# Attention with a sliding window, then a mixture of experts: the last tiles of the two expert lists as fixed slots

## Chip, cores, metric

The kernel runs on one core of a Trainium2 chip. The metric is the device time of one execution in microseconds. Engines: TensorE (PE; PEld is its weight load), VectorE (DVE), ScalarE (ACT), GpSimd (POOL), SyncE (SP, which here only issues DMAs).

## What is computed

```python
# q, k, v: [8, 8, 576, 64]; window 32; attention within |i - j| <= 32
scores = where(mask, q @ k.T / 8, -1e9)
x = softmax(scores) @ v              # -> [4608, 512], heads side by side
# mixture of experts: 8 experts, top 1, a bias for each of 2 modalities
logits = x @ w_gate + modality_bias[modality_id]
e_idx = argmax(logits, axis=1)
gate_w = softmax(logits)[e_idx]
for e in range(8):                   # w1[e]: 512 x 1024, w2[e]: 1024 x 512
    m = e_idx == e
    out[m] = gate_w[m] * (relu(x[m] @ w1[e]) @ w2[e])
```

The modality bias is much larger than the spread of `x @ w_gate`, so with these inputs one expert (list A below) gets 2308 rows and one (list B) 2300; the six others get none. The kernel holds for any distribution; it takes the two experts that the biases favour for its two lists.

## The kernel before

Nothing is scheduled by a compiler: the string `ORDER` lists every step of the program in the order in which it is emitted, and each engine executes its own steps in that order. A name is a step, the numbers are its batch and part, `/a`, `/v`, `/p` chooses ACT, DVE or POOL for a copy, and `:n` the PSUM banks.

For each of 8 batches: `l`, `lr`, `lv` load q and k (two groups of four heads, 512 KB each), the remainder rows and v, all but one by SyncE's queue; `c`, `cr`, `cv` cast to bf16; `TQ`, `TK`, `TR` transpose on PE and `tq`, `tk`, `tr` copy out of PSUM; `SA`, `SB` are the scores, `sa`, `sb` the exponentials, `M` the mask on DVE; `V` the product with v and `v` its normalisation into the tile `xt`. `X`, `x`, `L`, `lo`, `B`, `Q`, `E`, `R`, `P` compute the gate and the rank of each row in its expert's list; `Z` (five GpSimd indirect DMAs) scatters the batch's rows to the scratch `scr` in HBM, where each expert has a region of its own. `A` counts, after each batch, whether the two lists have filled another tile of 256 rows, and writes the row number `ri` of the two new tiles, 2b and 2b+1 (or that of a zero region).

`F` fetches a tile of 256 rows from `scr`: SyncE first loads `ri` into a register, then issues the DMA (the first four tiles go to `xg` and are transposed on PE by `N`; the later ones come by a transposing DMA to `xTf`, with a small one for `xm`). `U` (four groups of 8 matmuls) and `u` are the first product and its relu, `D` (two halves of 128 rows, 8 matmuls each) the second, `y` scales by the gate weight on DVE into one of four `ys` buffers, `O` stores rows by a GpSimd indirect DMA; `i` makes its row indices. `W` loads the weights of the two experts, each once.

After the eight batches 16 tiles (0 to 15) are planned, 2048 rows of each list, and 256 + 4 and 252 rows are left. `G`, 34 small DVE steps, makes a table of all remaining tiles of any expert; `J` (eight fills of 272 KB by SyncE's queue) zeroes the rows behind the end of each expert's region. Three more tiles (16, 17, 18) are always run from the table, with `C` before each: weight loads under a condition, on GpSimd's queue. Behind them a branch on the number of tiles in the table skips the code for 22 more. In these runs it is skipped.

Each GpSimd DMA is tracked by one of eight semaphores in turn. The span ends with the framework's own steps: semaphore increments for the DMAs in the skipped code, a drain of each engine, and a clearing of semaphores.

Of the kernel before, what the change touches and what calls it, by code (L numbers as in the profile page):

```python
# [37 lines left out]
tr1.1/v TQ5:7 tq5/v TQ6:2 sa3 lr2.0 TQ7:3 M2 sb3 tq6/v lr2.1 V2:45 tq7/a M3 SA4:67 SB4:01 sa4 l2.1.0 lv2.0 v2
cv1.0/p V3:23 sb4 l2.1.1 SA5:67 v3 cv1.2/p lv2.1 SB5:45 sa5 M4 sb5 X0.0:0 X0.1:1 X0.2:2 lv2.2 X0.3:3 X0.4:6
x0.0/v x0.1/a M5 x0.2/a lv2.3 x0.3/a lv2.4 x0.4/v c1.1.1/p cv1.1/a l3.0.0 c2.0.0/v L0:7 cr2/p c2.0.1/a V4:45  # L40
W0 lo0 l3.0.1 c2.1.0/v TK6:0 V5:12 tk6/a TK7:3 B0.0 lr3.0 TQ8:6 v4 tk7/a TK8:7 I0 TR2:0 tq8/a TQ9:3 B0.1 Q0.0
SA6:45 tk8/a lr3.1 B0.2 v5 TK9:6 E0 sa6 TQ10:7 l3.1.0 B0.3 Q0.1 SB6:12 tr2.0/a B0.4 Q0.2 SA7:45 tr2.1/a tq9/v
cv2.0/p sb6 R0:0 tk9/v TQ11:3 P0.0 sa7 M6 SB7:12 sb7 P0.1 V6:45 P0.4 P0.2 P0.5 tq10/a P0.3 A0.0 SA8:01 Z0.0 v6
tq11/a SB8:67 sa8 c2.1.1/v Z0.1 sb8 l3.1.1 TK10:2 Z0.2 TK11:3 tk10/a tk11/v Z0.3 Z0.4 A0.1 M7 A0.2 V7:45 M8
SA9:01 SB9:67 sa9 A0.3 v7 sb9 l4.0.0 A0.4 X1.0:2 A0.5 X1.1:3 X1.2:0 x1.0/a A0.6 l4.0.1 X1.3:1 x1.1/v X1.4:4
x1.2/a A0.7 x1.3/v x1.4/a M9 lr4.0 L1:5 lo1 cv2.1/p cv2.2/a c3.0.0/a B1.0 TQ12:6 Q1.0 c3.0.1/a TQ13:7 lr4.1 I1
B1.1 V8:23 tq12/v E1 V9:01 lv3.0 tq13/a B1.2 Q1.1 B1.3 SA10:45 Q1.2 TK12:6 cr3/a B1.4 F0 v8 TK13:7 sa10 v9
tk12/a c3.1.0/p R1:2 F1 SB10:34 tk13/a TR3:5 P1.0 sb10 tr3.0/v SA11:01 SB11:67 P1.1 P1.4 lv3.1 P1.2 P1.5
TQ14:2 sa11 P1.3 A1.0 TQ15:3 Z1.0 tr3.1/v N0:4 sb11 tq14/v n0/v Z1.1 tq15/a N1:5 c3.1.1/a Z1.2 U0.0:0 n1/v
cv3.0/a TK14:1 Z1.3 TK15:2 tk14/v U0.1:6 u0.0 Z1.4 tk15/v c4.0.0/a U0.2:7 lv3.2 A1.1 W1 U0.3:3 M10 u0.1 u0.2  # L50
TQ16:4 lv3.3 TQ17:5 A1.2 u0.3 M11 V10:01 Ke tq16/a lv3.4 SA12:67 SB12:23 sa12 A1.3 v10 D0.0.0:4 sb12 V11:67
A1.4 tq17/v SA13:01 c4.0.1/a D0.0.1 A1.5 v11 SB13:23 sa13 TK16:5 A1.6 y0.0 X2.0:6 sb13 X2.1:7 X2.2:0 A1.7
X2.3:1 x2.0/v X2.4:4 x2.1/a x2.2/v TK17:2 D0.1.0:3 x2.3/a x2.4/v tk16/a D0.1.1 M12 tk17/a L2:6 y0.1 lo2 M13 I2
cv3.1/a cv3.2/a U1.0:7 cr4/a F2 B2.0 V12:01 i0 u1.0 B2.1 V13:45 Q2.0 O0.0 l4.1.0 v12 E2 SA14:23 F3 SB14:67
sa14 O0.1 v13 SA15:01 l4.1.1 sb14 lv4.0 SB15:23 B2.2 Q2.1 l5.0.0 TR4:4 B2.3 U1.1:5 Q2.2 sa15 lv4.1 B2.4 M14
l5.0.1 R2:6 U1.2:7 u1.1 P2.0 sb15 tr4.0/v V14:01 P2.1 P2.4 U1.3:5 P2.2 P2.5 u1.2 P2.3 A2.0 SA16:23 Z2.0 v14
lv4.2 tr4.1/a N2:6 u1.3 D1.0.0:7 n2/a Z2.1 SB16:01 N3:4 sa16 Z2.2 U2.0:5 n3/v sb16 U2.1:6 Z2.3 lv4.3 c4.1.0/v
u2.0 D1.0.1 lr5.0 Z2.4 u2.1 TQ18:2 y1.0 TQ19:3 tq18/a U2.2:4 lv4.4 A2.1 tq19/a M15 D1.1.0:0 u2.2 lr5.1 U2.3:1
A2.2 M16 V15:56 u2.3 A2.3 SA17:23 i1 D1.1.1 A2.4 sa17 v15 O1.0 D2.0.0:7 cv4.0/a A2.5 y1.1 SB17:12 X3.0:4
X3.1:3 sb17 A2.6 X3.2:5 x3.0/v O1.1 X3.3:6 X3.4:0 D2.0.1 x3.1/v x3.2/a A2.7 U3.0:4 x3.3/a y2.0 x3.4/a U3.1:1  # L60
M17 u3.0 L3:2 F4 u3.1 i2 U3.2:3 c4.1.1/p lo3 cv4.1/a cv4.2/v D2.1.0:5 B3.0 I3 i3 u3.2 B3.1 F5 Q3.0 O2.0 V16:67
c5.0.0/a c5.0.1/v TK18:0 V17:12 E3 B3.2 tk18/a l5.1.0 v16 TK19:4 TQ20:3 lv5.0 tk19/a D2.1.1 l5.1.1 B3.3 tq20/a
Q3.1 SA18:67 B3.4 lv5.1 TK20:0 y2.1 sa18 TQ21:4 l6.0.0 TK21:3 Q3.2 lv5.2 v17 O2.1 tk20/a R3:5 SB18:67 tq21/a
U3.3:0 P3.0 i4 sb18 lv5.3 P3.1 P3.4 SA19:12 P3.2 U4.0:4 l6.0.1 P3.5 P3.3 u3.3 A3.0 M18 SB19:56 lv5.4 u4.0
D3.0.0:7 sa19 A3.1 U4.1:0 tk21/v Z3.0 lr6.0 sb19 cr5/v V18:12 A3.2 TR5:4 i5 u4.1 D3.0.1 A3.3 v18 Z3.1 tr5.0/a
lr6.1 SA20:56 tr5.1/a U4.2:3 sa20 Z3.2 y3.0 l6.1.0 SB20:01 u4.2 cv5.0/v D3.1.0:4 Z3.3 sb20 U4.3:2 c5.1.0/v
# [42 lines left out]
def kernel(  # L109
# [12 lines left out]
    nc = tc.nc  # L122
# [25 lines left out]
    ctx.enter_context(tc.manual_schedule())  # L148
# [869 lines left out]
```

## Time and profile before

| | |
|---|---|
| median of 3 runs | 308.91 us (305.42 to 310.55) |
| the profiled execution | 306.1 us, its span 304.4 us |
| mean granted TensorE clock | 0.904 |
| PE, DVE, ACT, POOL busy | 230.8, 169.1, 165.7, 106.7 us |
| DMA moved | 55.11 MB |

Durations in the text are from the profiled execution. Windows list the busy time of each engine, TensorE's granted clock, the mean busy share of the 16 DMA engines and GB/s. In a timeline the number in brackets is how long the engine stood idle before an instruction, and behind the arrow is what ended the wait; "issue" means nothing that the profile shows. Lines with SPq, POOLq and so on are those of an engine's sequencer.

### The profile page before, as it was taken

To read this page: it belongs to the slowest core of one execution; us is meant where nothing else is said; L and a number is where in the kernel's file an instruction comes from. 1 tells how busy PE (TensorE), PEld (TensorE's weight loads), DVE (VectorE), ACT (ScalarE), POOL (GpSimd) and SP (SyncE) were. 2 spreads that over 40 slices of the span, in tenths; PEclk is the share of its full clock that TensorE was granted. 3 is DMA by queue.
4 is the path that set the end of the run, shared out by engine and by line. 5 is a ranking of instruction groups with operands and counts; after the bars stand their busy time and mean duration, and the time that the engine had idled before them with its cause. 6 is when DMAs were issued, how large, how long until landed. Compare 5 with 4: busy or idle time off the path is not lost. (4 is left out here: it accounts for less than half of the span.)

```text
span 304.4 us, 6737 instructions
## 1 busy us (share of the span) xinstructions
PE 230.8 (76%) x2497; PEld 165.1 (54%) x2497; DVE 169.1 (56%) x486; ACT 165.7 (54%) x287; POOL 106.7 (35%) x150
## 2 busy tenths in 40 slices
PE   0087785671897989996996995999999399999700
PEld 0065573561775667764773773677756166666300
DVE  7168887852587467865874774677651742321200
ACT  0396978574497478859885974675331133233100
POOL 6012264516402513372135236131447422322300
PEclk9999978657699799999999799799999789999955
DMA  5999999999998965999999642062055887410110
GB/s 172 211 266 261 261 245 203 289 301 218 236 197 228 323 164 124 257 304 320 231 212 302 167 89 105 37 91 86 34 96 148 296 269 140 138 73 32 75 40 1
DMA packets 95171, 55.11 MB, mean 181 GB/s; under 512 B 68851, under 2 KB 90651, under 8 KB 95131
## 3 DMA queue, kind: packets, MB, share of 16 engines
q1 hardware_dynamic: 85835, 35.42, 52.6%
q0 software_dynamic: 8624, 18.66, 21.6%
q10 hardware_dynamic: 672, 0.53, 0.5%
q8 instruction: 21, 0.34, 0.5%
q14 instruction: 19, 0.16, 0.2%
HBM read 50.49 MB, written 18.04 MB: 225 GB/s over the span
## 5 line engine op out<-in xcount | busy, mean ns | idle before, releaser
L803 PE MATMUL banks<-xTf,w 128*128 128x256 bf16 x608 | 79.3, 280 | 5.1 <-issue 5.0
L809 ACT ACTIVATE hT<-banks 128x512 bf16<-128x512 f32 x76 | 45.1, 601 | 63.9 <-PE banks L803 53.1
L816 PE MATMUL banks<-w,hT 128*128 128x512 bf16 x304 | 76.3, 386 | 2.4 <-ACT hT L809 1.9
L830 POOL DMA_INDIRECT out_dram<-ys,ix x38 | 39.2, 1033 | 96.2 <-DVE ys L823 24.7
L803 PEld LDWEIGHTS <-w 128*128 128x128 bf16 x608 | 59.0, 100 | 18.0 <-issue 5.5
L522 ACT ACTIVATE pt<-banks 128x768 bf16<-128x768 f32 x64 | 50.7, 823 | 18.3 <-PE banks L514 14.8
L676 POOL DMA_INDIRECT scr<-xt,di x40 | 41.7, 1042 | 35.6 <-issue 29.9
L823 DVE TENSOR_SCALAR ys<-banks,xm 128x512 f32<-128x512 f32 x30 | 22.5, 750 | 46.0 <-PE banks L816 31.0
L816 PEld LDWEIGHTS <-hT 128*128 128x128 bf16 x304 | 28.3, 99 | 31.3 <-ACT hT L809 3.8
L482 PE MATMUL banks<-ident,cb 128*128 128x128 bf16 x256 | 25.9, 260 | 25.0 <-ACT cb L187 23.4
L536 DVE TENSOR_TENSOR pt<-pt,mask 128x1920 bf16<-128x1920 bf16 x32 | 36.8, 1151 | 1.8 <-ACT pt L525 1.8
L482 PEld LDWEIGHTS <-cb 128*128 128x128 bf16 x256 | 20.4, 118 | 30.2 <-ACT cb L187 24.1
L514 PE MATMUL banks<-qT,kT 64*128 64x192 bf16 (+1 forms) x320 | 24.6, 263 | 7.7 <-DVE kT L189 2.4
L550 PE MATMUL banks<-vt,pt 128*128 128x65 bf16 x320 | 24.9, 205 | 5.9 <-DVE pt L536 4.6
L550 PEld LDWEIGHTS <-pt 128*128 128x128 bf16 x320 | 23.1, 106 | 8.7 <-DVE pt L536 5.5
L565 DVE TENSOR_TENSOR xt<-banks,rec 128x640 bf16<-128x640 f32 x32 | 26.4, 824 | 1.6 <-DVE rec L564 0.4
L555 PE MATMUL banks<-vt,pt 128*128 128x65 bf16 x256 | 23.8, 205 | 0.0
L514 PEld LDWEIGHTS <-kT 64*128 64x128 bf16 x320 | 12.6, 101 | 16.9 <-issue 11.0
L555 PEld LDWEIGHTS <-pt 128*128 128x128 bf16 x256 | 20.4, 105 | 0.6 <-issue 0.5
L187 ACT CAST cb<-qkf 128x1024 bf16<-128x1024 f32 x17 | 17.6, 1063 | 2.6 <-DMA qkf<-in_k_dram 1.5
L187 ACT COPY kT<-banks 128x512 bf16<-128x512 bf16 (+1 forms) x29 | 15.3, 554 | 4.6 <-PE banks L482 3.5
L189 DVE COPY qT<-banks 128x512 bf16<-128x512 bf16 (+1 forms) x16 | 9.7, 610 | 14.4 <-PE banks L482 12.4
(159 smaller groups left out, 231.0 us busy)
## 6 DMA issues: line engine op xcount, KB each, us to landing
w<-in_moe_w_dram POOLq DMA_DIRECT2D x10, 1024.0 KB
qkf<-in_q_dram SPq DMA_DIRECT2D x16, 512.0 KB
vf<-in_v_dram SPq DMA_DIRECT2D x32, 256.0 KB
qkf<-in_k_dram SPq DMA_DIRECT2D x15, 512.0 KB
scr<-zero SPq DMA_DIRECT2D x9, 272.0 KB
xg<-scr SPq DMA_DIRECT2D x4, 272.0 KB
rf<-in_q_dram SPq DMA_DIRECT2D x8, 128.0 KB
rf<-in_k_dram SPq DMA_DIRECT2D x8, 128.0 KB
```

The lines of the kernel that those rows point to most:

```text
L187: nc.scalar.copy(o_ap, i_ap)
L482: nc.tensor.transpose(tp[:, i, :], Ct["c", b, hp // 2, u][:, i, D * l_:D * l_ + P], ident[:])
L514: nc.tensor.matmul(st[:, h, c0:c0 + w_], k_t[b % 2][D * h:D * h + D, hp, P * j:P * j + P], q_t[b % 2][D * h:D * h + D, hp, P * j:P * j + w ...
L522: nc.scalar.activation(p_ap, st[:, :, 0:2 * WIN].rearrange("p h (j c) -> p h j c", c=WIN), ACT.Exp, scale=scale)
L536: masked.append(nc.vector.tensor_tensor(out=p_ap, in0=p_ap, in1=mask[:].unsqueeze(1).to_broadcast([P, 2 * NM, WIN]), op=ALU.mult))
L550: nc.tensor.matmul(o_ap, pt[:, h, SW * m:SW * m + P], vt[:, m, 2 * hp + h, :], start=(m == 0), stop=(m == 0), skip_group_check=True)
L555: nc.tensor.matmul(o_ap, pt[:, h, c1:c1 + P], vt[:, m - 1, 2 * hp + h, :], start=False, stop=True, skip_group_check=True)
L676: ins = nc.gpsimd.indirect_dma_start(out=scr[:], out_offset=bass.IndirectOffsetOnAxis(ap=Ct["di", b][:, m:m + 1], axis=0), in_=x_t[b % 2][ ...
L803: nc.tensor.matmul(ph[:, u, :], w1_sb[t % 2][:, kd, P * mi:P * mi + P], Ct["N", t][1][:, kd, :], start=(kd == 0), stop=(kd == n_kd - 1))
L809: nc.scalar.activation(Ct["h", t][:, 2 * mp:2 * mp + 2, :], Ct["U", t, mp][:, :, :], ACT.Relu)
L816: nc.tensor.matmul(Ct["D", t, s], Ct["h", t][:, kf, P * s:P * s + P], w2_sb[t % 2][:, kf, :], start=(kf == 0), stop=(kf == n_kf - 1))
L830: ins = nc.gpsimd.indirect_dma_start(out=out, out_offset=bass.IndirectOffsetOnAxis(ap=Ct["i", t][:, s:s + 1], axis=0), in_=Ct["y", t, s][: ...
```

## The change

The order is written anew throughout. Six things change beside it.

1. Tiles 16, 17 and 18 become fixed slots: 16 is the next 256 rows of list A, 17 the next of list B, 18 a tile of 128 rows, again of list A. `A` carries list A a second time for it, and ten DVE steps, `H`, make row numbers and penalties. No weights are loaded for them.
2. The table `G` serves only the branch, which is taken if any row is left. Only two fills `J` stand ahead of it; eight more are inside.
3. In the branch, the way taken when no tile is left is laid out differently (`preferred_fallthrough_block`).
4. `k` is a drain of GpSimd. It stands at eight places on GpSimd's queue: ahead of O2.0, Z3.1, the copy I4, O8.0, O10.1, O13.0, O14.0 and O16.0.
5. A one-element exponential on ACT stands at the start (`warm`).
6. In the first batch q and k are loaded ahead of v.

```diff
-Kp0 lv0.0 lr0.0 Kb lv0.1 lr0.1 lv0.2 l0.1.0 Kx cv0.0/a c0.0.0/a lv0.3 l0.1.1 Kp1 Ka TQ0:0 TQ1:1 c0.0.1/a Km Kc
...
-D17.0.0:1 y16.1 C18 D17.0.1 O16.1 D17.1.0:3 y17.0 U18.0:2 O17.0 U18.1:0 u18.0 U18.2:5 u18.1 U18.3:6 u18.2
+Kp0 lr0.0 lr0.1 Kb Kx c0.0.0/a l0.1.0 Kp1 Ka TQ0:0 TQ1:1 tq0/a c0.0.1/p tq1/a l0.1.1 cr0/a Km Kc TK0:2 TK1:3
...
+u17.2 k16 U17.3:6 D16.1.1 u17.3 D17.0.0:4 y16.1 O16.0 U18.0:2 O16.1 U18.1:3 u18.0 D17.0.1 u18.1 D17.1.0:1
...
-    N_TAIL = 3
+    T_A, T_B, T_C = 2 * B, 2 * B + 1, 2 * B + 2
...
+    warm = const.tile([P, 1], FP32)
+    nc.vector.memset(warm[:], 0.0)
+    nc.scalar.activation(warm[:], warm[:], ACT.Exp)
...
     def A(_, b, i):
         if i == 0:
-            nc.vector.tensor_tensor(out=rtile(("cm", b), [P, 2, E])[:], in0=oh_ab[:],
-                                    in1=base[:].unsqueeze(1).to_broadcast([P, 2, E]), op=ALU.mult)
+            nc.vector.tensor_tensor(out=rtile(("cm", b), [P, 3, E])[:], in0=oh_ab[:],
+                                    in1=base[:].unsqueeze(1).to_broadcast([P, 3, E]), op=ALU.mult)
...
     def F_(_, t):
...
+        elif t <= T_C:
+            row_ap = T["rl"][0:1, t - T_A:t - T_A + 1]
+            deps = [i_ for _, i_ in scr_ins] + fill_ins + zp_ins
         else:
-            row_ap = T["tab"][0:1, 2, t - 2 * B:t - 2 * B + 1]
-            deps = [i_ for _, i_ in scr_ins] + fill_ins + zp_ins if t < 2 * B + N_TAIL else None
+            row_ap = T["tab"][0:1, 2, t - T_C - 2:t - T_C - 1]
+            deps = None
         r_r = reg(row_ap, [ET.SP], 0, ZP)
-        rows = scr[bass.ds(r_r, TT), :]
+        ns = 1 if t == T_C else 2
+        rows = scr[bass.ds(r_r, P * ns), :]
...
     def U(_, t, mp):
-        ph = bank([P, 2, TT])
-        for u in range(2):
-            mi = 2 * mp + u
+        nu, w_ = (4, P) if t == T_C else (2, TT)
+        ph = bank([P, nu, w_])
+        for u in range(nu):
+            mi = nu * mp + u
             for kd in range(n_kd):
-                nc.tensor.matmul(ph[:, u, :], w1_sb[t % 2][:, kd, P * mi:P * mi + P], Ct["N", t][1][:, kd, :],
-                                 start=(kd == 0), stop=(kd == n_kd - 1))
+                nc.tensor.matmul(ph[:, u, :], w1_sb[t % 2][:, kd, P * mi:P * mi + P],
+                                 Ct["N", t][1][:, kd, 0:w_], start=(kd == 0), stop=(kd == n_kd - 1))
...
+    def last_tiles():
+        ca = Ct["ca", B - 1]
+        end_i = const.tile([P, 2], I32)
+        nc.vector.tensor_tensor(out=end_i[:], in0=row_ab[:, 0:2], in1=ca[:, 0:2], op=ALU.add)
...
+        T["rl"] = rl
...
+        T["pl"] = pen_l
...
+    op["H"] = lambda _, i_: next(last_steps)
...
+    def fill(row_ap):
+        r_e = reg(row_ap, [ET.SP], 0, ZP - TT)
+        return nc.sync.dma_start(scr[bass.ds(r_e, TT), :].rearrange("(s p) c -> p s c", p=P), zero[:])
...
+    op["k"] = lambda _, i_: nc.gpsimd.drain()
...
-    with tc.If(n_tiles > N_TAIL, preferred_fallthrough_block=False):
-        for t in range(2 * B + N_TAIL, 2 * B + NTILE):
-            tile_alone(t)
+    with tc.If(n_tiles > 0, preferred_fallthrough_block=True):
+        for e in range(E):
+            fill(T["ends"][0:1, e:e + 1])
+        for i_ in range(NTILE):
+            tile_alone(T_C + 2 + i_)
```

How the instructions move at three places (x4 behind a row is a run of equal rows). SyncE's queue at the start of the program, before: q of the first four heads, then v and the remainder rows (`rf`) in turn, then q and k of the other four heads. (k of the first four goes by ACT's queue in both kernels.)

```order
L225 DMA qkf<-in_q_dram 128x4x256
L265 DMA vf<-in_v_dram 128x8x64
L241 DMA rf<-in_q_dram 64x8x64
L265 DMA vf<-in_v_dram 128x8x64
L241 DMA rf<-in_k_dram 64x8x64
L265 DMA vf<-in_v_dram 128x8x64
```

And now:

```order
L226 DMA qkf<-in_q_dram 128x4x256
L242 DMA rf<-in_q_dram 64x8x64
L242 DMA rf<-in_k_dram 64x8x64
L226 DMA qkf<-in_q_dram 128x4x256
L226 DMA qkf<-in_k_dram 128x4x256
L307 DMA mid_106<-in_moe_modality_id_dram 8x96
L308 DMA mid_106<-in_moe_modality_id_dram 24x1x128
L309 DMA mid_106<-in_moe_modality_id_dram 8x96
L266 DMA vf<-in_v_dram 128x8x64 x4
```

All loads of v moved behind q, k and the modality ids.

SyncE's queue around the fetch of tile 0, the first that reads `ri`; before, q, k and remainders of batch 3 stand ahead of it (the last rows before it):

```order
L225 DMA qkf<-in_q_dram 128x4x256
L225 DMA qkf<-in_k_dram 128x4x256
L241 DMA rf<-in_q_dram 64x8x64
L241 DMA rf<-in_k_dram 64x8x64
L265 DMA vf<-in_v_dram 128x8x64
L182 TENSOR_LOAD ri
L755 ISA
L755 DMA xg<-scr 128x2x272
```

And now:

```order
L226 DMA qkf<-in_q_dram 128x4x256
L226 DMA qkf<-in_k_dram 128x4x256
L266 DMA vf<-in_v_dram 128x8x64 x3
L183 TENSOR_LOAD ri
L771 ISA
L771 DMA xg<-scr 128x2x272
```

The q and k here are the second half of batch 2, so the fetch of tile 0 moved ahead of all of batch 3.

GpSimd's queue at the branch, before: if it isn't taken, the engine falls into the increments (ISA) and then jumps over the code of the 22 tiles.

```order
L830 DMA out_dram<-ys,ix 4608x512 x5
L984 TENSOR_LOAD tab
L986 COMPARE_AND_BRANCH
L986 ISA
L986 UNCONDITIONAL_BRANCH
L182 TENSOR_LOAD tab x2
```

And now, with the last two rows of the branch's code and what follows it:

```order
L851 DMA out_dram<-ys,ix 4608x512 x2
L1055 UNCONDITIONAL_BRANCH
L1055 ISA
L1055 UNCONDITIONAL_BRANCH
L1085 ISA
```

The increments moved behind the code of the tiles: the jump over it comes first.

More of the change, by code (lines that the diff above doesn't have):

```diff
@@ L38 @@
[L38 to L42, printed above, removed]
@@ L422 @@
     ext_e = const.tile([P, NTILE + 2], FP32)
-    oh_ab = const.tile([P, 2, E], FP32)
-    row_ab = const.tile([P, 2], FP32)
+    oh_ab = const.tile([P, 3, E], FP32)
+    row_ab = const.tile([P, 3], FP32)
     sp_i = const.tile([P, 2], I32)
+    df = const.tile([P, 1], FP32)
     @named
@@ L450, in Kx @@
                                 scalar2=None, op0=ALU.add)
-        nc.vector.tensor_scalar(out=row_ab[:], in0=ext_e[:, 0:2], scalar1=float(LP), scalar2=None, op0=ALU.mult)
+        nc.vector.tensor_scalar(out=row_ab[:, 0:2], in0=ext_e[:, 0:2], scalar1=float(LP), scalar2=None, op0=ALU.mult)
         nc.vector.tensor_copy(sp_i[:], ext_e[:, 0:2])
@@ L847, in table @@
         dn = const.tile([P, E], FP32)
-        nc.vector.tensor_scalar(out=thr[:], in0=thr[:], scalar1=-float(TT), scalar2=None, op0=ALU.add)
-        yield
-        nc.vector.tensor_tensor(out=dn2[:], in0=oh_ab[:], in1=thr[:].unsqueeze(2).to_broadcast([P, 2, E]), op=ALU.mult)
+        nc.vector.tensor_tensor(out=dn2[:], in0=oh_ab[:, 1:3, :],
+                                in1=T["th"][:, 1:3].unsqueeze(2).to_broadcast([P, 2, E]), op=ALU.mult)
         yield
@@ L952 @@
     op["G"] = lambda _, i_: next(steps)
+    def fill(row_ap):
+        r_e = reg(row_ap, [ET.SP], 0, ZP - TT)
+        return nc.sync.dma_start(scr[bass.ds(r_e, TT), :].rearrange("(s p) c -> p s c", p=P), zero[:])
     @named
     def J(_, e):
-        r_e = reg(T["end"][0:1, e:e + 1], [ET.SP], 0, ZP - TT)
-        ins = nc.sync.dma_start(scr[bass.ds(r_e, TT), :].rearrange("(s p) c -> p s c", p=P), zero[:])
+        ins = fill(T["end"][0:1, e:e + 1])
         unordered(ins, "scr")
```

200 lines of the change are left out of this document (122 added, 78 removed).

## The prediction

> **What bounds the kernel now.** I read the page first, then the windows, the timelines of the stretches where TensorE stands still, and last the rows of the end.
>
> ```profile
> PE 230.8 (76%) x2497; PEld 165.1 (54%) x2497; DVE 169.1 (56%) x486; ACT 165.7 (54%) x287; POOL 106.7 (35%) x150
> ...
> 20.00:40.00 20.00, 14.75 (x213) 11.77 (x212) 17.49 (x31) 16.85 (x29) 3.84 (x5) 1.00 1.12 262
> 60.00:80.00 20.00, 10.02 (x112) 8.23 (x113) 7.64 (x25) 10.53 (x17) 10.69 (x23) 0.63 1.14 268
> ...
> 110.00:115.00 5.00, 5.00 (x56) 3.50 (x55) 4.31 (x11) 3.45 (x8) 0.95 (x1) 1.00 0.13 31
> 170.00:175.00 5.00, 5.00 (x58) 3.93 (x57) 3.15 (x14) 4.24 (x9) 1.16 (x2) 0.91 0.37 105
> 235.00:240.00 5.00, 2.03 (x11) 0.90 (x10) 2.69 (x8) 0.60 (x1) 3.78 (x5) 0.91 0.99 295
> 240.00:245.00 5.00, 2.49 (x8) 0.85 (x8) 4.52 (x22) 2.06 (x4) 0.41 (x1) 0.50 0.68 254
> 290.00:295.00 5.00, 0.00 (x0) 0.00 (x0) 0.00 (x0) 0.00 (x0) 0.00 (x0) 0.53 0.09 34
> ...
> 283.67 3.40 PE L816 MATMUL banks<-w,hT 128*128 128x512 bf16 x15
> ```
>
> The window rows give PE, PEld, DVE, ACT, POOL, then granted clock, DMA share and GB/s. TensorE is busy for 230.8 of 304.4 us, so 73.6 us are idle, and the question is where they lie. They have four homes. Up to 15.8 us nothing has reached TensorE. From there to 170 us, where their share falls to 0.37, the DMA engines are the limit (1.12 and 1.14 in the two windows shown), except around 110 us, where their share falls to 0.13 while loads are still outstanding. After 170 us TensorE is nearly always busy, except in 235 to 245 us: 4.5 of 10. Behind the last matmul, which ends near 287.1 us, come some 17 us without any engine. The profiled execution took 306.1 us, 1.7 beyond its span and 2.8 below the median of 308.91.
>
> **The end.** These are instructions of GpSimd's sequencer.
>
> ```profile
> 288.13 0.97 POOL L830 DMA_INDIRECT out_dram<-ys,ix  x1 [0.69 <-DVEq L986]
> ...
> L986 POOLq EVENT_SEMAPHORE  x5: 17/43/43, 288.6 to 291.5; - x5
> L986 POOLq INC_SWDGE_SEM  x1: 1847/1847/1847, 292.1 to 292.1; - x1
> L986 POOLq COMPARE_BRANCH  x2: 41/44/48, 288.5 to 294.0; - x2
> ...
> L1013 POOLq DRAIN  x3: 46/103/6903, 296.7 to 304.1; - x3
> L1002 POOLq DRAIN  x1: 183/183/183, 0.5 to 0.5; - x1
> ...
> scr<-xt,di POOLq DMA_INDIRECT x40
> out_dram<-ys,ix POOLq DMA_INDIRECT x38
> w<-in_moe_w_dram POOLq DMA_DIRECT2D x10, 1024.0 KB
> wg_sb<-in_moe_w_gate_dram POOLq DMA_DIRECT2D x1, 8.0 KB
> ```
>
> The last store is issued at 288.1 and has landed by 291.5; then 1.85 us in INC_SWDGE_SEM, a jump at 294.0 and nothing until 296.7, and a drain of 6.9 us. The data are long in memory by then: it is not a transfer that this drain waits for. A drain with nothing before it takes 0.18 us, and the two behind the long one at most 0.10. So I read it as bookkeeping for each DMA that GpSimd issued since the last drain: 40 + 38 + 10 and one for the gate weights make 89, that is 78 ns each (83, if six weight loads that their condition skipped don't count). The changed kernel drains eight times on the way, the last time behind the stores of tile 15, with five stores to follow: 5 x 78 = 0.4 us, **6.5 saved** (bounds: nothing, if the drain has a fixed price, and 6.9). If INC_SWDGE_SEM walks the same list, it falls to about 0.5, 1.3 saved (0 to 1.8). The jump's 2.6 us now come before the wait for the last landing instead of behind it, and that wait is 2.4 us long (289.1 to 291.5): 2.0 saved (0 to 2.6). Together **-9.8**, between 0 and -11.3.
>
> The Trainium skill ("Runtime: NRT & Kernel Launch", "Instruction fetch mechanics") says that a taken branch to a page outside the fetch window must first fetch it; the 2.6 us behind the jump agree. By that rule alone both kernels make one far jump and the 2.0 would be lost, a sum 2.0 us higher; I keep it, since the new one has a wait to hide behind.
>
> **The half tile.** Of 2308 and 2300 rows, 16 tiles take 2048 each. What is left, 256 + 4 and 252, was three tiles of 256 and becomes two, and one of 128.
>
> ```profile
> 279.09 3.66 PE L803 MATMUL banks<-xTf,w 128*128 128x256 bf16 x32
> 275.64 3.62 PE L816 MATMUL banks<-w,hT 128*128 128x512 bf16 x16
> L482 PE MATMUL banks<-ident,cb 128*128 128x128 bf16 x256 | 25.9, 260 | 25.0 <-ACT cb L187 23.4 <-DVE cb L189 1.2 <-POOL cb L191 0.4
> 45.02 0.62 PE L482 MATMUL banks<-ident,cb 128*128 128x128 bf16 x8
> 276.71 0.05 POOL L722 DMA_DIRECT2D w<-in_moe_w_dram  x1 [2.95 <-DMA w<-in_moe_w_dram]
> ```
>
> The second product drops 8 of 16 matmuls: 1.8 us. The first keeps 32, on 128 columns instead of 256. A pair of that size comes every (0.62 - 0.26) / 7 = 51 ns (the group's mean of one, 260 ns, for the first), so 1.7 to 1.9 us instead of 3.66. **-3.6**, in a stretch where TensorE has no idle time; its price if the weight loads don't keep up is bounded by no gain on the first product, -1.8. The weight loads that were skipped by condition cost GpSimd a wait of 2.95 us, but TensorE's matmuls go on across it: 0.
>
> The Trainium skill ("TensorE: Matmul & The Clock Gate", "Back-to-back issue gap") gives about 81 ns for such a pair in a sustained stream; its estimate would be 32 x 81 = 2.6 us, and the term -2.9. The row of this trace is faster than that, and decides.
>
> **The stall at 235 us.**
>
> ```profile
> 237.86 9.30 SPq L958 DMA_DIRECT2D scr<-zero  x8
> 240.73 0.37 PE L803 MATMUL banks<-xTf,w 128*128 128x256 bf16 x1 [1.83 <-issue]
> 235.79 0.75 DVE L823 TENSOR_SCALAR ys<-banks,xm 128x512 f32<-128x512 f32 x1 [6.08 <-DMA out_dram<-ys,ix]
> ```
>
> Eight fills of 272 KB go out in 9.3 us. In the same stretch TensorE issues the matmuls of one group with over a microsecond between them and waits for nothing visible, as if its instructions came late over the full DMA engines, and DVE waits 6.1 us for a `ys` buffer, because the stores stand behind GpSimd's scatters. Two fills remain, and the table's 34 DVE steps no longer precede a fetch. The scatters stay in front of the stores. Of 5.5 idle us I take 3.5 back: **-3.5** (0 to -5.5).
>
> **The first phase.**
>
> ```profile
> 12.48 1.28 ACT L187 ACT_TABLE_LOAD   x1 [12.48 <-DMA vf<-in_v_dram]
> ...
> 14.73 1.99 ACT L187 CAST cb<-qkf 128x1024 bf16<-128x1024 f32 x2
> 15.82 1.98 PE L482 MATMUL banks<-ident,cb 128*128 128x128 bf16 x16 [15.82 <-ACT cb L187]
> ...
> 4.00:6.00 2.00, 0.00 (x0) 0.00 (x0) 1.61 (x12) 0.00 (x0) 1.86 (x9) 1.00 0.99 324
> 6.00:8.00 2.00, 0.00 (x0) 0.00 (x0) 1.81 (x12) 0.00 (x0) 0.52 (x3) 1.00 1.23 291
> ...
> 56.77 0.17 DVE L701 TENSOR_SCALAR ri<-ro 128x2 int32<-128x2 f32 x1
> 69.42 3.95 SPq L755 DMA_DIRECT2D xg<-scr  x2
> 75.86 1.04 PE L785 MATMUL banks<-ident,xg 128*128 128x128 bf16 x8 [6.42 <-DMA xg<-scr]
> ...
> 106.82 0.70 SPq L241 DMA_DIRECT2D rf<-in_k_dram  x1
> 115.33 0.16 DVE L701 TENSOR_SCALAR ri<-ro 128x2 int32<-128x2 f32 x1
> 116.39 1.37 SPq L760 DMA_TRANSPOSE xTf<-scr  x1
> ```
>
> ScalarE's first work is a cast of v, whose loads land at 12.5; only then do the table load, that cast and the q cast follow. Now q and k come first, 1.05 MB, and at the 290 to 320 GB/s of 4 to 8 us they are there near 8; the table load lies ahead of them. First transposes near 9 instead of 15.8: 6.8 us. The row of tile 0 is known at 56.8, but its fetch stands behind four more q and k loads and their remainders in SyncE's queue and starts at 69.4; TensorE waits 6.4 us for it. In the new queue only three v loads separate it from the loads of its own batch's successor. Around 110 us the queue stands for 9.6 us at the fetch of tile 4, until DVE has made its row number at 115.3, with no load behind it going out.
>
> None of these three adds up freely, since the DMA engines set this stage: a TensorE that starts 6.8 us earlier meets the same arrival of v, and a fetch put forward pushes a load back. What can stay is expert work done inside the phase. The new order holds one batch fewer of loads ahead of the fetch of tile 4, so the queue can run dry there again. Of 6.8 + 6.4 + 9.6 = 22.8 I take about a quarter: **-6**; bounds +6 (a prefetch too shallow, three more stops of about 2 us) and -21.
>
> **The drains on the way.**
>
> ```profile
> 284.68 0.97 POOL L830 DMA_INDIRECT out_dram<-ys,ix  x1 [4.19 <-DVE ys L823]
> ```
>
> A drain should wait for what is in flight (2.4 us for a store at the end) and then pay 78 ns per entry: about 3.3 us for eleven. GpSimd is busy for 35%, and in the last tiles it waits 4.2 us between two tiles' stores, so four of the eight, in front of the stores of tiles 10, 13, 14 and 16, are nearly covered. Queued behind a drain are those stores; behind them DVE's `ys` buffers, then the PSUM banks, then TensorE. I set **+3** (0 to +9). DVE's wider lists (24 elements for 16) and ten small steps at 0.16 us lie beside TensorE's work: 0; without that cover 2 us.
>
> **Sum.** 306.1 - 9.8 - 3.6 - 3.5 - 6 + 3 = 286.2 for a profiled run; with the 2.8 between that and the median, **289.0**.
>
> **Rivals.**
> - The loads decide less than I think, and all of the first phase comes through: -21 instead of -6 gives 274. For it speaks TensorE's idle time there, 5 and 10 us in the two windows shown; against it the DMA share. Chance 0.14.
> - The end doesn't move, because the last drain's price has another cause, and the first phase keeps its length: 308.9 - 3.6 - 3.5 - 2 = 300. Against it: 0.05 to 0.18 us for drains with nothing before them. Chance 0.14.
> - The shallower prefetch starves the DMA engines: +6 instead of -6, and the drains at +6: about 304. For it: one empty stretch already in the old order. Chance 0.12.
> - Slower: a drain costs its 6.9 us each time, however little is queued. It decides once a drain exceeds the 4 us that GpSimd has free between two tiles: with 2.4 of landing, the four late ones expose about 5 us each on TensorE, and the end keeps its 6.5: 289 + 6.5 + 20 - 3 = 312. Against it speak the same short drains; but none with few entries is in the trace. Chance 0.08.
>
> My forecast, 282 to 297, has 0.52. The range must leave out no more than two in ten: the slow case, a part of the starved one and a part of the good first phase, so 276 to 303. Faster by over 2% (6.2 us, under 302.7; about what a measurement of this kernel tells from none): 0.52 + 0.14 + 0.12 of the second case + 0.02 of the third = 0.80. Within 2%: 0.12. Slower: 0.08.
>
> **What would show it.** GpSimd's last drain under 1 us, the drains on the way about 3 us each, and less than 9 us behind the last matmul: the end. First matmul near 9 us. The fetch of tile 0 before 65 us. No window after 200 us with TensorE under 4 of 5 us. DMA share above 0.8 in every window until the last load, and that load by about 165 us: the first phase. I am wrong if a drain on the way takes over 5 us, if stores wait behind them while TensorE stands, or if SyncE's queue stands longer at a fetch than before.

## The result and the profile after

The changed kernel takes **284.43 us** (median of 4 runs, 280.99 to 287.43) beside 308.37 for the kernel before (4 runs, 305.42 to 310.55): a ratio of 0.9216 [0.9079, 0.9352]. The forecast was 289.0 (276 to 303). The profiled execution took 284.0 us (span 282.3, granted clock 0.927), 22.1 less than that of before. The ratios here and below leave disturbed, slower executions out and the medians do not, so the two can differ by a per cent; the profiles of e2, e3 and e4 below come from such executions.

Where the time went is read from four stretches of both kernels: up to the first matmul, to 170 us, to the end of the last matmul, and behind it. (170 us is the same time and not the same place in the program: the changed kernel has issued 1638 matmuls by then, the one before 1536.) The columns are the stretch, its length and the busy time of PE, PEld, DVE, ACT and POOL, then the granted clock, the DMA share and GB/s. First before, then after.

```profile
0.00:15.82 15.82, 0.00 (x0) 0.00 (x1) 6.67 (x39) 3.33 (x4) 5.30 (x28) 1.00 1.01 195
15.82:170.00 154.18, 123.20 (x1536) 92.17 (x1537) 104.08 (x264) 112.59 (x196) 56.92 (x71) 0.89 1.06 248
170.00:287.07 117.07, 107.56 (x964) 72.88 (x962) 57.56 (x183) 49.83 (x89) 43.12 (x51) 0.95 0.42 113
287.07:304.40 17.33, 0.00 (x0) 0.00 (x0) 0.75 (x1) 0.00 (x0) 1.34 (x2) 0.59 0.09 34
```

```profile
0.00:7.08 7.08, 0.00 (x0) 0.00 (x1) 5.21 (x34) 2.53 (x3) 1.94 (x13) 1.00 0.55 164
7.08:170.00 162.92, 130.58 (x1638) 96.10 (x1639) 116.87 (x298) 116.32 (x202) 72.66 (x94) 0.93 1.05 248
170.00:275.03 105.03, 94.15 (x855) 64.32 (x852) 53.91 (x170) 43.02 (x76) 38.43 (x40) 0.94 0.39 109
275.03:282.30 7.27, 0.00 (x0) 0.00 (x0) 0.75 (x1) 0.00 (x0) 1.33 (x2) 0.75 0.13 43
```

Length minus PE is TensorE's idle time. It falls by 8.7 us ahead of the first matmul (15.8 to 7.1) and by 10.1 behind the last (17.3 to 7.3). Between them it does not fall at all: it rises from 31.0 to 32.3 in the second stretch and from 9.5 to 10.9 in the third, 2.7 together. TensorE's work falls by 6.0 (PE 230.8 to 224.7 us), of which the half tile is some 3.5. That is 8.7 + 10.1 - 2.7 + 6.0 = 22.1.

The end, in GpSimd's sequencer, and the last two groups of matmuls:

```profile
270.55 4.48 PE L837 MATMUL banks<-w,hT 128*128 128x512 bf16 x20
268.76 1.95 PE L823 MATMUL banks<-xTf,w 128*128 128x128 bf16 x32
L1055 POOLq EVENT_SEMAPHORE  x5: 17/42/43, 280.0 to 280.3; - x5
L1055 POOLq COMPARE_BRANCH  x1: 61/61/61, 276.5 to 276.5; - x1
L1055 POOLq INC_SWDGE_SEM  x1: 296/296/296, 280.4 to 280.4; - x1
L1085 POOLq DRAIN  x3: 46/103/455, 280.8 to 282.0; - x3
```

The last drain takes 0.455 us where it took 6.903, INC_SWDGE_SEM 0.296 for 1.847. The branch at 276.5 now stands ahead of the wait for the last store, and nothing far follows it. The 32 matmuls on 128 columns take 1.95 us.

The first phase, from the timelines of the engines:

```profile
7.08 1.03 PE L493 MATMUL banks<-ident,cb 128*128 128x128 bf16 x8 [7.08 <-ACT cb L188]
54.37 1.32 SPq L771 DMA_DIRECT2D xg<-scr  x2
127.94 0.87 SPq L226 DMA_DIRECT2D qkf<-in_q_dram  x1
142.97 1.28 SPq L776 DMA_TRANSPOSE xTf<-scr  x1
141.99 0.16 DVE L713 TENSOR_SCALAR ri<-ro 128x2 int32<-128x2 f32 x1
173.66 0.66 SPq L264 DMA_DIRECT2D vl<-in_v_dram  x1
```

TensorE starts at 7.1 instead of 15.8, the fetch of tile 0 goes out at 54.4 instead of 69.4. But SyncE's queue now stands at the fetch of tile 6 from 128.8 to 143.0, 14.2 us (before, 9.6 at that of tile 4), until DVE has made the row number at 142.0, and the last load is issued at 173.7, not by 165.

And the windows in which TensorE still stands:

```profile
135.00:140.00 5.00, 0.89 (x10) 0.40 (x10) 1.70 (x4) 1.55 (x3) 2.58 (x3) 0.88 0.46 172
210.00:215.00 5.00, 2.36 (x15) 1.32 (x15) 2.16 (x5) 1.08 (x2) 2.15 (x3) 0.89 0.27 101
230.00:235.00 5.00, 2.42 (x15) 1.30 (x14) 0.00 (x0) 0.60 (x1) 3.78 (x5) 0.93 0.66 232
```

### The profile page after: what moved, and what is told of

Its sections match the earlier page's. It is cut to its first block, busy times and chain, and to the rows that moved or that the text cites. A ratio compares the mean times of both kernels' runs of the same rounds, so it can differ in the third digit from the quotient of the medians.

```text
span 282.3 us, 6657 instructions
## 1 busy us (share of the span) xinstructions
PE 224.7 (80%) x2489; PEld 160.4 (57%) x2489; DVE 176.7 (63%) x500; ACT 161.9 (57%) x281; POOL 114.4 (41%) x148
## 5 line engine op out<-in xcount | busy, mean ns | idle before, releaser
L823 PE MATMUL banks<-xTf,w 128*128 128x256 bf16 (+1 forms) x608 | 77.3, 279 | 1.7 <-issue 1.5
L837 PE MATMUL banks<-w,hT 128*128 128x512 bf16 x296 | 74.2, 383 | 5.2 <-issue 3.3
L830 ACT ACTIVATE hT<-banks 128x512 bf16<-128x512 f32 x74 | 43.6, 599 | 58.5 <-PE banks L823 41.6
L533 ACT ACTIVATE pt<-banks 128x768 bf16<-128x768 f32 x64 | 50.7, 821 | 22.3 <-PE banks L525 10.4
L687 POOL DMA_INDIRECT scr<-xt,di x40 | 43.6, 1090 | 31.4 <-issue 25.0
L493 PE MATMUL banks<-ident,cb 128*128 128x128 bf16 x256 | 22.6, 236 | 19.0 <-ACT cb L188 8.9
L561 PE MATMUL banks<-vt,pt 128*128 128x65 bf16 x320 | 23.7, 204 | 10.1 <-DVE pt L547 8.8
L493 PEld LDWEIGHTS <-cb 128*128 128x128 bf16 x256 | 17.0, 105 | 23.5 <-ACT cb L188 9.2
L566 PE MATMUL banks<-vt,pt 128*128 128x65 bf16 x256 | 22.9, 204 | 0.0
L525 PEld LDWEIGHTS <-kT 64*128 64x128 bf16 x320 | 13.1, 103 | 15.1 <-issue 12.4
L192 POOL TENSOR_SCALAR cb<-qkf 128x1024 bf16<-128x1024 f32 x11 | 12.1, 1101 | 17.3 <-DVE pt L547 7.3
L575 DVE RECIPROCAL rec<-banks 128x10 f32<-128x10 f32 x32 | 6.9, 215 | 19.4 <-PE banks L566 11.3
L188 ACT COPY qT<-banks 128x512 bf16<-128x512 bf16 (+1 forms) x26 | 13.9, 560 | 7.8 <-PE banks L493 5.1
```

The source lines that it names most:

```text
L493: nc.tensor.transpose(tp[:, i, :], Ct["c", b, hp // 2, u][:, i, D * l_:D * l_ + P], ident[:])
L525: nc.tensor.matmul(st[:, h, c0:c0 + w_], k_t[b % 2][D * h:D * h + D, hp, P * j:P * j + P], q_t[b % 2][D * h:D * h + D, hp, P * j:P * j + w ...
L533: nc.scalar.activation(p_ap, st[:, :, 0:2 * WIN].rearrange("p h (j c) -> p h j c", c=WIN), ACT.Exp, scale=scale)
L561: nc.tensor.matmul(o_ap, pt[:, h, SW * m:SW * m + P], vt[:, m, 2 * hp + h, :], start=(m == 0), stop=(m == 0), skip_group_check=True)
L566: nc.tensor.matmul(o_ap, pt[:, h, c1:c1 + P], vt[:, m - 1, 2 * hp + h, :], start=False, stop=True, skip_group_check=True)
L687: ins = nc.gpsimd.indirect_dma_start(out=scr[:], out_offset=bass.IndirectOffsetOnAxis(ap=Ct["di", b][:, m:m + 1], axis=0), in_=x_t[b % 2][ ...
```

## The experiments

Three groups of runs on three chips. Shares are of the kernel before on the same chip. On the third chip everything is faster, the kernel before at 285.5 us instead of 308 to 311; there the changed kernel ran once more as a control, with the share that it had before (0.924 and 0.922), though not in the 281 to 288 us expected. Between groups only shares are compared, and even these may move by a per cent or two from chip to chip (see e6).

| run | edit | median us | share of before, 95% |
|---|---|---|---|
| e1, 1st chip | changed, no drains | 295.9 | 0.968 [0.963, 0.974] |
| e2, 1st | before, with drains | 307.0 | 0.990 [0.984, 0.996] |
| e3, 1st | before, two fills | 311.7 | 1.003 [0.997, 1.009] |
| e4, 1st | changed, four more drains | 280.8 | 0.915 [0.910, 0.920] |
| e5, 2nd | changed, loads ahead | 288.5 | 0.937 [0.927, 0.946] |
| e6, 2nd | changed, v first | 291.7 | 0.949 [0.939, 0.958] |
| e7, 2nd | changed, full last tile | 292.5 | 0.950 [0.942, 0.958] |
| e8, 2nd | e4 and e5 | 279.8 | 0.910 [0.902, 0.918] |
| e9, 3rd | changed | 264.3 | 0.924 [0.918, 0.930] |
| e10, 3rd | changed, four pauses | 268.9 | 0.941 [0.935, 0.947] |
| e11, 3rd | e8, one cast to ScalarE | 271.6 | 0.952 [0.947, 0.958] |
| e12, 3rd | changed, one drain | 260.9 | 0.914 [0.909, 0.919] |

### What the drains do to the end: e1, e2, e12

Changed, without drains; before, with drains; changed, with the last drain alone (entries of the written order):

```diff
 e1:  -k2 -k4 -k6 -k8 -k10 -k12 -k14 -k16
 e2:  c4.1.1/p +k2 ... Z3.0 +k4 ... O4.0 +k6 ... O7.1 +k8 ... I7 +k10 ... O11.1 +k12 ... O13.1 +k14 ... O15.1 +k16
 e12: -k2 -k4 -k6 -k8 -k10 -k12 -k14    (k16 stays)
```

> The changed kernel with its eight drains on the way left out. Theory A (a drain pays about 78 ns for each DMA that GpSimd issued since the last one): some 80 entries are left for the last drain, which takes 6.2 us or more instead of 0.46, and INC_SWDGE_SEM about 1.8 instead of 0.30, so the end grows by about 7; the drains held GpSimd for about 2 us each behind its last work and cost at most 3 on the path, so 284.4 becomes 288 to 291.5. Theory B (the end was short for another cause, such as the jump that now lies ahead of the last wait): the last drain stays under 1 us and the time falls by up to 3, to 281.5 to 284.4. A third statement, on the standstills of all engines near 135, 178, 212 and 233 us: if the drains make them, they go; if trains of more than five indirect DMAs make them, they stay.

> The kernel before with eight drains at the same places among the scatters and stores of GpSimd, nothing else changed. Theory A (a price for each DMA since the last drain): the last drain falls from 6.9 to under 1 us, INC_SWDGE_SEM from 1.85 to about 0.4, so 308.4 becomes 301 to 304 (minus 7.5, plus 0 to 3 for the drains). Theory B: the drains add their 2 us each where GpSimd is waited for, the end stays; 308 to 315. The far jump stays behind the last wait here, so this kernel's end keeps 2 us that the changed one has lost.

> The changed kernel with one of its eight drains, the last, ahead of the stores of tile 16; seven are left out. Bookkeeping for each DMA, 82 ns from the two ends measured (5 in 0.455 us, 82 in 6.77): the drain on the way takes 6 to 9 us, the last one 0.455 as in the changed kernel, INC_SWDGE_SEM 0.30. It lies where GpSimd has 3 to 4 us free between two stores, so up to 5 us come onto the path there; and the trains that the seven drains broke stay whole. Time 3 to 8 above the changed kernel, and below the 295.9 of the kernel without any drain. If a drain had a fixed price: the one on the way takes 3 us and the time is at or below the changed kernel's.

The drains of e1, of e2, of the full tile e7 (six stores behind its last drain on the way) and of e12, in GpSimd's sequencer (the three numbers are the shortest, the median and the longest, in ns; e12 with the two stores on either side of its drain):

```profile
L1084 POOLq DRAIN  x3: 46/103/6773, 286.4 to 293.8; - x3
L1054 POOLq INC_SWDGE_SEM  x1: 1836/1836/1836, 284.5 to 284.5; - x1
```

```profile
L1015 POOLq DRAIN  x3: 46/103/592, 307.7 to 308.9; - x3
L988 POOLq INC_SWDGE_SEM  x1: 307/307/307, 304.7 to 304.7; - x1
```

```profile
L1084 POOLq DRAIN  x3: 46/103/537, 288.7 to 289.9; - x3
```

```profile
L1030 POOLq DRAIN  x1: 7577/7577/7577, 238.1 to 238.1; - x1
238.34 0.97 POOL L850 DMA_INDIRECT out_dram<-ys,ix  x1 [2.43 <-DVE ys L843]
246.55 0.97 POOL L850 DMA_INDIRECT out_dram<-ys,ix  x1 [7.24 <-issue]
L1084 POOLq DRAIN  x3: 46/103/465, 256.6 to 257.9; - x3
```

A drain's price is one for each DMA since the last: 5 cost 0.455 us, 6 cost 0.537, 82 cost 6.773, that is **82 ns each** and some 45 ns besides. (The 6.903 of before, for 89, says that the six weight loads that were skipped count for next to nothing.) In e12 the one drain pays for 77 at once, 6.4 us behind its last store, while GpSimd alone stands: the four `ys` buffers carry TensorE across it. The rival in which a drain has a fixed price falls.

The other half of what was expected failed. e1's end grows by 7.5 us as foreseen (14.8 behind the last matmul instead of 7.3), but its time, 295.9, lies above the 288 to 291.5 expected: the drains on the way were taken for a cost of up to 3 us, and by the shares (0.968 against 0.922) leaving them out loses some 6 us more than the end, an estimate between groups. The end of e2 falls as foreseen, yet the whole by only 1.0% [0.4, 1.6], about 3 us: at those places in the old order the drains give back some 5. Its jump still stands behind the last wait, and its end is 8.8 us, 1.5 longer than that of the changed kernel. And e12 is no slower than the control, as was expected, but **faster**: 260.9 beside 264.3. On that chip seven of the eight drains cost 3.4 us and bring nothing, since the last one alone makes the end short.

### The standstills: e3, e4, e9, e10

e3 leaves fills 0 and 4. e4 adds a drain, e10 a pause, behind the third scatter of four batches.

```diff
 e3:  -J1 -J2 -J3 -J5 -J6 -J7
 e4:  Z3.2 +k23 ... Z5.2 +k25 ... Z6.2 +k26 ... Z7.2 +k27
 e10: Z3.2 +q23 ... Z5.2 +q25 ... Z6.2 +q26 ... Z7.2 +q27    (q: two GpSimd casts of 128x1024, unused)
```

> The kernel before with two of its eight fills left, those at the ends of the two lists that these inputs use; rows behind other lists are not filled. My forecast's theory (the fills keep the DMA engines full, so that TensorE's instructions come late near 235 us): the standstill of 5.5 us in 235 to 245 shrinks to 2 or less, 308.4 becomes 303 to 305.5. Rival (the standstill comes from GpSimd's train of eleven indirect DMAs from 226.5 to 240.4, and ends when the train ends): it stays at 4 to 6 us and the time within 1.5 us of 308.4.

> The changed kernel with four more drains, one behind the third scatter of batches 3, 5, 6 and 7, which break trains of seven and eight indirect DMAs into at most five. Theory T (while GpSimd issues indirect DMAs without a pause for more than some 6 us, the other engines run out of instructions until the train ends): the standstills that start 6 to 7 us behind a train's start (near 135, 178, 212 and 233 us; 4, 4, 4 and 2.5 us) shrink to under 1 us each, 284.4 becomes 274 to 280. Theory S (the stores stand behind the scatters, and DVE's four ys buffers run out): each drain makes the stores 2 us later, the standstills stay or grow, 285 to 292. Theory N (they are chance or come from elsewhere): within 2 of 284.4.

> The changed kernel as it is, beside the others of this group: a control, since the experiments before it ran on other days and chips than it did. 281 to 288; its share of the time before 0.912 to 0.935.

> The changed kernel with four pauses of GpSimd of 2.1 us (two casts of 128x1024 that nobody uses) behind the third scatter of batches 3, 5, 6 and 7, where the kernel with short trains had four more drains. Theory T1 (the other engines starve when GpSimd issues indirect DMAs for more than some 6 us without a break, and any break of 2 us lets them go on): the standstills near 212 and 233 us shrink from 1.7 and 2.2 us with all engines idle to under 0.7, and the time is 2 to 5 below the changed kernel's. Theory T2 (it is the drain that helps, because it waits until what was issued has landed): they stay, and the time is the changed kernel's, or up to 3 above it.

The windows run from the start of a train of indirect DMAs to just behind its end. Before, and e3:

```profile
226.50:242.00 15.50, 10.90 (x71) 6.66 (x69) 6.93 (x33) 1.55 (x3) 10.82 (x11) 0.91 0.79 223
```

```profile
230.80:247.00 16.20, 9.16 (x60) 5.69 (x59) 7.32 (x34) 1.21 (x3) 10.72 (x11) 0.92 0.70 196
```

With a quarter of the fills TensorE stands for 7.0 us of this stretch instead of 4.6, and the time is the same. **The fills were not its cause.** Now the trains (GpSimd's indirect DMAs without a break, seven and eight of them) of batches 6 and 7: changed, e4, and the changed kernel on the third chip.

```profile
203.50:214.50 11.00, 8.80 (x91) 6.16 (x88) 5.33 (x14) 3.46 (x8) 7.26 (x8) 0.97 0.30 106
225.50:236.00 10.50, 7.92 (x60) 5.72 (x59) 2.87 (x19) 2.39 (x4) 7.77 (x8) 0.92 0.65 207
```

```profile
205.80:219.00 13.20, 12.54 (x145) 9.48 (x146) 8.07 (x24) 5.66 (x11) 7.28 (x8) 1.00 0.25 90
224.10:239.00 14.90, 14.35 (x100) 9.75 (x100) 4.82 (x22) 4.67 (x8) 8.76 (x9) 1.00 0.60 170
```

```profile
193.50:204.00 10.50, 10.39 (x116) 8.12 (x117) 7.36 (x19) 4.94 (x10) 7.26 (x8) 1.00 0.31 111
210.90:222.00 11.10, 11.05 (x84) 8.14 (x84) 4.20 (x21) 4.78 (x8) 7.78 (x8) 1.00 0.68 213
```

Two trains, TensorE idle: 2.2 and 2.6 us as changed, 1.9 and 2.9 in e1 (8.90 busy of 10.80 and 8.93 of 11.80 us), so the drains do not make these standstills; 0.7 and 0.6 with a drain inside each train, although those drains hold GpSimd longer. That is against theory S (stores behind scatters). But on the third chip the same instructions, seven and eight in a train without a break, leave 0.1 and 0.1, and e12, with the same two trains, leaves the same. So a long train is not enough; the standstill belongs to a train and to a chip, as far as one trace of each run can say. What makes the difference stays open. e10 cannot tell a pause from a drain, since on its chip there was nothing to shrink; its pauses cost 4.6 us, and TensorE waits 3.7 us for a cast of v that stands behind the train.

In time e4 does not settle it alone: 280.8 lies above the 274 to 280 of theory T, and 0.915 [0.910, 0.920] is not clearly below the changed kernel's 0.922 [0.908, 0.935]. Against e1, on the same chip, the drains were worth much: e4 with twelve is 15.1 us faster than e1 with none, 7.5 of it the end. Which of the twelve bring the other 7.6 was not taken apart.

### The first phase: e5, e6, e8, e11

```diff
 e5:  +l4.1.0 +l4.1.1 +lv4.0 +lv4.1 F4 ... +l6.1.1 +lv6.0 +lv6.1 +lv6.2 +lv6.3 +lv6.4 +l7.0.0 F6    (taken from behind them)
 e6:  Kp0 +lv0.0 lr0.0 Kb +lv0.1 lr0.1 +lv0.2 l0.1.0 Kx +cv0.0/a c0.0.0/a +lv0.3 l0.1.1 ... +lv0.4
 e8:  e4 and e5
 e11: e8, and -cv5.2/p +cv5.2/a
```

> The changed kernel with loads moved ahead of two fetches at which SyncE's queue stands: two q and k loads and two v loads ahead of the fetch of tile 4 (queue stands 89.9 to 96.1 us), seven loads ahead of the fetch of tile 6 (128.8 to 143.0 us). Theory A (loads still set this stage, and the stops waste DMA time): both stops are filled, the last load is issued near 163 instead of 173.7, and 284.4 becomes 276 to 281. Theory B (TensorE, GpSimd's trains and the scatters set this stage, the loads have slack): the loads come earlier and the time stays within 2 of 284.4. Slower, if the fetch then waits behind the loads: up to 288.

> The changed kernel with the start of the one before: the five v loads of batch 0 go out among the first q and k loads and ScalarE's first work is the cast of v; the rest is as changed. TensorE's first matmul moves from 7.1 to 13 to 16 us. Theory A (the earlier start survives, since TensorE's own work sets the first 60 us): 284.4 becomes 290 to 294. Theory B, my forecast's (the DMA engines set the stage, v arrives as before, most of the earlier start is given back): 284.4 to 287. The tile fetches say where it is given back: the fetch of tile 0 at 54.4 moves by as much as survives until there.

> The changed kernel with both: the loads ahead of the two fetches, and four more drains that break GpSimd's trains of indirect DMAs (these alone gave 0.915 of the time before, against 0.922 for the changed kernel). If the two act in different places they add up: 281 less what the loads give, 272 to 279. If the loads have slack: 280 to 282. If loads packed more densely make the scatters and drains slower: above 284.

> The kernel with both edits (loads ahead, four more drains) and one cast moved: the remainder of v of batch 5 is cast by ScalarE instead of GpSimd, where it stood behind five scatters and stores while TensorE waited 7.0 us for it (141 to 148 us). If that wait is a wait for this cast: it shrinks to under 2 us there, and the time falls from 279.8 (0.910 of before) by 3 to 5, to 275 to 277. If the train of indirect DMAs holds TensorE there anyway: no change, 278 to 282.

The start of e6 and its fetch of tile 0, and of e7, whose start is as changed, on the same chip:

```profile
14.57 1.89 PE L492 MATMUL banks<-ident,cb 128*128 128x128 bf16 x16 [14.57 <-ACT cb L187]
58.16 1.32 SPq L770 DMA_DIRECT2D xg<-scr  x2
268.12 1.91 PE L822 MATMUL banks<-xTf,w 128*128 128x256 bf16 x16
```

```profile
8.31 1.03 PE L492 MATMUL banks<-ident,cb 128*128 128x128 bf16 x8 [8.31 <-ACT cb L187]
56.10 1.34 SPq L770 DMA_DIRECT2D xg<-scr  x2
267.02 1.91 PE L822 MATMUL banks<-xTf,w 128*128 128x256 bf16 x16
```

A start that is 6.3 us later makes the fetch 2.1 later, and the same group of tile 17 only 1.1 later. Most of it is given back, as forecast (theory B); medians put the loss at 2.7 (291.7, beside 292.5 less the 3.4 of the full tile, 289.1), at the edge of theory B's band. The changed kernel itself did not run on that chip. By its share elsewhere it would take 283 to 288 us there, an estimate by which e6 loses 4 to 8, as theory A had it. I go by e7: up to the group of tile 17 it is the changed program, and it gets there at 267.0 us where the changed kernel's own trace has 261.8, so on this chip that program takes some 5 us more than 284.

SyncE's queue in e5, around the fetches of tile 6 and of tile 8:

```profile
140.41 0.57 SPq L225 DMA_DIRECT2D qkf<-in_q_dram  x1
149.81 1.28 SPq L775 DMA_TRANSPOSE xTf<-scr  x1
158.04 5.09 SPq L265 DMA_DIRECT2D vf<-in_v_dram  x3
173.57 2.09 SPq L775 DMA_TRANSPOSE xTf<-scr  x1
```

e5 shortens the stop at tile 6 to 8.8 us (14.4 in e7), but the queue then stands 10.4 at the fetch of tile 8, where e7's stands 0.7, and the last load goes out no earlier (179.3, in e7 178.7). The time, 288.5, is that of the estimate just made. So putting these loads ahead gains nothing. Whether the stage would be shorter with all loads earlier (theory A) or not (theory B), e5 cannot tell, since its loads did not end earlier. e8, 279.8 us, is 8.7 faster than e5 on the same chip, by its four drains; its time is the one foreseen if the loads add nothing to them (280 to 282). e11 shows what a drain can hold up where loads are dense (a DMA share of 0.95 to 1.17 from 130 to 145 us), on the third chip:

```profile
131.44 0.98 POOL L686 DMA_INDIRECT scr<-xt,di  x1 [0.30 <-issue]
138.89 0.97 POOL L686 DMA_INDIRECT scr<-xt,di  x1 [6.47 <-issue]
146.26 1.08 POOL L191 TENSOR_SCALAR cb<-qkf 128x1024 bf16<-128x1024 f32 x1
147.40 1.89 PE L492 MATMUL banks<-ident,cb 128*128 128x128 bf16 x16 [7.89 <-POOL cb L191]
```

The drain holds GpSimd for 6.5 us; scatters, stores and a cast of the next batch stand behind it, and TensorE waits 7.9 us for that cast. I had moved one cast out of the way, and the next one took its place. The share, 0.952, is worse than the changed kernel's 0.924 on that chip, where a gain of 3 to 5 us over e8 or none was expected. e8 itself did not run there, so what the moved cast does is not separated from what the drains and loads of e8 do on this chip.

### The half tile: e7

```diff
-        ns = 1 if t == T_C else 2
+        ns = 2
-        nu, w_ = (4, P) if t == T_C else (2, TT)
+        nu, w_ = 2, TT
 ... D17.0.1 +U18.2:0 u18.1 D17.1.0:1 y17.0 +U18.3:5 +u18.2 D17.1.1 +u18.3 ... +D18.1.0:4 y18.0 +D18.1.1 O18.0 +y18.1 +O18.1
```

> The changed kernel with its last tile at 256 rows again: 32 matmuls of the first product on 256 columns and 16 of the second, one store more. Theory A (no idle time in that stretch): the tile's matmuls take 3.66 instead of 1.95 us and another 1.8 us, 284.4 becomes 287.5 to 288.5, and GpSimd's last drain 0.53 instead of 0.455 us. Rival (the stores or DVE set the end): 284.4 to 286.

From the group of tile 17 shown above to the end of the last matmul, e7 takes 16.65 us (267.02 to 283.67) and e6, with the half tile, 13.21 (268.12 to 281.33): **3.4**, where 3.6 were forecast. The median of e7 has no control on its chip, but lies at 4.0 above that of e5.

## Why the prediction was right

**The end: right, by its own steps.** -9.8 forecast, -10.1 measured: 6.4 of the last drain, 1.6 of INC_SWDGE_SEM, and 2.1 that fit the jump moved ahead of the wait. The price for each DMA was taken as 78 ns and is 82; e1 puts 7.5 us back at the end by leaving the drains out, and nothing else. The jump's part was not taken back by itself; e2, which keeps the old jump, ends 1.5 longer.

**The half tile: right**, -3.6 against 3.4. The row of the trace was the better guide: the Trainium skill ("TensorE: Matmul & The Clock Gate", "Back-to-back issue gap") has about 81 ns for a pair, and 32 took 1.95 us, 61 ns each, a little more than the 1.7 to 1.9 forecast.

**The stall at 235 us: wrong.** -3.5 was forecast. The step that failed is the reading that eight fills keep TensorE's instructions back. Six fills went, and in their place TensorE idles 2.6 us in the train of batch 7 and 2.2 in that of batch 6: after 170 us it stands for 10.9 us instead of 9.5. Two windows after 200 us have TensorE at 2.4 of 5, against the mark of 4. e3 shows that the fills alone bring nothing.

**The first phase: right in size, not in its picture.** -6 forecast; the idle time up to 170 us falls by 7.4. The earlier start came, and e6, beside e7, shows that most of it is given back. But the shallower prefetch that I held for a rival is there as well, in the 14.2 us at the fetch of tile 6, by the mark that I had set for being wrong: the DMA share falls to 0.46 in 135 to 140 us, and the last load goes out at 173.7, not by 165. What the stop costs stays open: e5 puts loads ahead of it and gains nothing, but its queue then stands at the next fetch. That the DMA engines set the stage, the reason given for taking only a quarter, is not shown. What the order gained otherwise up to 170 us was not taken apart.

**The drains on the way: +3, and the sign depends on the place and the chip.** On the third chip seven of them cost 3.4 us, and in e2's order eight cost about 5. On the first chip, in the new order, the drains on the way gain (e4 against e1). In the trace of the changed kernel GpSimd stands 3.73 us at one of them, behind the first scatter of batch 3 (the last row is e8's):

```profile
L1031 POOLq DRAIN  x8: 2257/4332/8718, 94.1 to 261.9; - x8
...
127.85 0.97 POOL L687 DMA_INDIRECT scr<-xt,di  x1 [3.73 <-issue]
137.27 0.65 POOL L192 TENSOR_SCALAR vt<-vl 64x512 bf16<-64x512 f32 x1
138.35 0.22 DVE L575 RECIPROCAL rec<-banks 128x10 f32<-128x10 f32 x1 [3.27 <-remote]
139.49 0.50 PE L525 MATMUL banks<-qT,kT 64*128 64x192 bf16 x4 [3.97 <-DVE xt L576]
```

```profile
148.03 0.21 PE L560 MATMUL banks<-vt,pt 128*128 128x65 bf16 x1 [6.97 <-POOL vt L191]
```

The drains' own rows read 2.3 to 8.7 us, but those hold the queued DMAs that a drain waits for; the mark "over 5 us" was set on the wrong number. In 135 to 140 us TensorE works 0.89 of 5, but not for want of the cast of v that stands behind that train: it waits 3.97 us for DVE, whose own wait of 3.27 us is put down to nothing on this core ("remote"), and ACT stands 4.58 us by "issue". Both go on a microsecond behind the train's last store, which ends at 137.3. That is a standstill like those after 200 us, and DVE's row number for tile 6, at 142.0, comes behind it; on the third chip, in the same kernel, the queue stands 8.1 us at that fetch instead of 14.2. In e8, with one more drain in the train, TensorE does wait 6.97 us for this very cast. A cast on GpSimd's queue behind a drain was not in my list of who is waited for.

**What was not in the sum:** 2.6 us less TensorE time beside the half tile, at a granted clock of 0.927 instead of 0.904 (the 256 transposes of q and k alone take 22.6 us instead of 25.9). The sum came out 2.2 us above the profiled time: work (2.4 more than forecast went), the first phase (1.4) and the end (0.3) outdid the 1.9 by which the stall and the drains together were missed. Part of it is luck, then: two terms were wrong and covered. Of the 22.1 us, runs or rows give 10.1 to the end, 3.4 to the half tile and 2.7 to the earlier start; the other 6 or so lie in the order, the drains and the clock, and stay open. The 2.8 between profile and median, added on top, was not there (284.0 and 284.4).

## What to carry to other kernels

Where a kernel ends in a long drain, count the DMAs that the engine issued, and put one drain late, where its queue has slack and buffers cover it: one did as much for the end as eight, and on the chip where both ran it was faster than the changed kernel (0.914 of before against 0.924). One alone was not run on the chips where drains among the scatters gain. A drain on the way also holds casts and stores queued behind it, so read what stands behind it before placing it. An idle stretch that lies beside a busy DMA engine is not yet caused by it: take the transfers away and look whether it goes.

## What was not expected of the hardware

- One chip ran the kernel before in 285.5 us where the others took 308 to 311, and the changed one without the standstills in the long trains of GpSimd's indirect DMAs of batches 6 and 7: 0.1 us of TensorE idle per train against 2.2 and 2.6. Drains among the scatters shrink them on the first chip; on the one without them seven drains cost 3.4 us.
- A drain in the middle of the stage in which loads fill the DMA engines holds GpSimd for 3.7 to 6.5 us, while its few entries, at 82 ns, come to under 0.5. It ends once the scatters have landed, as I read it: in e11 one of the two ahead of the drain, issued at 129.4, needs 7.8 us to land. The last of the eight, behind a few stores, holds it for 1.9 (3.14 us from 261.9, the store ahead of it ending at 263.2).
